# Moving the short VectorE operations of weight scales and negated maxima two steps back, behind the bank that VectorE empties

## The chip, the cores and the metric

The kernel runs on one core of a Trainium2 chip. A core has five engines with queues of their own: PE (TensorE, matrix multiplication), DVE (VectorE), ACT (ScalarE), POOL (GpSimd) and SP (SyncE, which here issues nearly all DMAs). Matmuls write into PSUM, which has eight banks; the other engines copy results from there to SBUF. The metric is the time of one execution on the device in microseconds (us). The kernel before takes 827.7 us, the median of three runs (827.12 to 828.55).

## What is computed

A layer norm, then attention with a sliding window of 256 tokens over 32 heads of 16 values, times a gate that a SwiGLU feed-forward network makes of the same normalised tokens. There are 2048 tokens of 512 values; the hidden size of the network is 1792.

```python
xn = layernorm(x)                                  # 2048 x 512
q, k, v = split(xn @ wqkv)                         # 32 heads of 16
scores = q @ k.T * 16**-0.5                        # masked: 0 <= i - j < 256
s = (softmax(scores) @ v) @ wo
g = silu((silu(xn @ w1) * (xn @ w3)) @ w2)
out = x + s * g
```

## The kernel before

Tokens are worked in four blocks of 512 (t), heads in four groups of eight (g), each group in two pairs of column sets (p): 32 units (t, g, p). Precision comes from splitting each fp32 operand into a high and a low fp16 part and summing three products (high by high, low by high, high by low). So that the fp16 parts lie in range, each weight matrix is first scaled by a power of two. The work around that scale is what the change touches:

- `squares` (L226) sums the squares of a weight tile, on ACT (L235) or DVE (L237), and casts the sums (L247).
- `powers` (L258) adds them over partitions with small matmuls (L271) into a spare part of a scores bank and returns `rest`: two operations (L280, L281) that read this bank, and three (L283, L287, L289) that make of the sum a power of two and its inverse, on tiles of 128 x 1 or 128 x 4.
- `then` (L292) runs that `rest` and what follows from it: L822 and L823 for a pair of gate and up weights, L870 to L876 for a group of down weights, where L876 writes the scale `sw`.
- With the scale known, `split_pool` (L313) cuts the raw weight: ACT scales it (L314) and casts the high part (L315), POOL subtracts for the low part (L311), in two halves. The result is stored to DRAM on SP's queue (L906, L956) for the later blocks of tokens, which load it again (L800, L846).

Attention runs in two passes. `pass1` (L605) computes scores with PE (L623) and takes their maxima on DVE (L637); after its last batch it negates the maxima of the unit into `NM` in two halves (L642, L643). `finish` (L648) later transposes these on PE (L652), DVE copies them out (L658), and SP writes them beside the queries. `pass2` (L678) computes the scores again, now with the negated maximum as two more rows (L699), adds the masks on DVE (L706), takes exponentials on ACT (L709), multiplies with the values (L727); DVE copies the sums out of PSUM (L742, L743). The denominators go through DRAM (L749, L750) and come back with the DMA of L764; DVE inverts them (L768, L769).

The dense work runs between the batches: projections (L567, emptied by L576 on ACT and L580 on DVE), gate and up products (L900, emptied by L915 on ACT, L919 and L924 on DVE), down products (L950, emptied by L974), the output product (L1001). All dense products share two PSUM banks, m0 and m1, so PE starts the next one when DVE has emptied the one before the last.

What sets the order: PE's instructions run in the order in which the kernel emits them. On the other engines a scheduler orders them by dependencies and priority when the kernel is built; each engine then runs its list strictly in order. `later(n, f)` queues the function f for n steps on; a step is counted after each batch of attention and each dense piece. `urgent` raises the priority of operations that empty PSUM. `tc.issue_after(x)` holds what it encloses behind instruction x in the list. `lasts["emptied"]` is the operation with which DVE last emptied a dense bank at the time of emission (L580, L919, L924, L971, L974 or L1005). `squares` already places its cast behind that one. Memory slots are given out in the order of the steps, so a step that is moved can change which slot a later tile gets.

Of the kernel before, what the change touches and what calls it, by code (L numbers as in the profile page):

```python
# [15 lines left out]
ALU = mybir.AluOpType  # L16
# [31 lines left out]
ONE = 2.0**12  # L48
# [31 lines left out]
def tile_block(ctx: ExitStack, tc: tile.TileContext, x, wqkv, wo, w1, w3, w2, out):  # L80
    nc = tc.nc
# [52 lines left out]
    def urgent():  # L134


        return tc.high_priority(offset=200) if started else nullcontext()
    made_so_far = [0]

    def later(n, f):  # L140
        made_so_far[0] += 1
        queue.append((now[0] + n, made_so_far[0], f))
# [21 lines left out]
    def scores_bank():  # L164

        return pss.tile([P, 2, 512], F32, name="s")
# [91 lines left out]
    def powers(sb, n, p2, inv, s=None):  # L258


        m = sb.shape[-1] // n
        al = small.tile([P, n], F32, name="al")
        if s is None:
            ps = scores_bank()[:, 0, 0:n]
            for i in range(m):
                nc.tensor.matmul(ps, onesb, sb[:, i * n:(i + 1) * n], start=i == 0, stop=i == m - 1)
        else:
            for h in range(2):
                for c in range(2):
                    for i in range(m):  # L270
                        nc.tensor.matmul(s[64 * c:64 * c + 64, h, WIN:WIN + n],  # L271
                                         onesb[64 * h:64 * h + 64, 64 * c:64 * c + 64],
                                         sb[64 * h:64 * h + 64, i * n:(i + 1) * n], start=i == 0, stop=i == m - 1)

        def rest():
            if s is None:
                nc.vector.tensor_scalar(al, ps, 2.08, 1e-30, op0=ALU.mult, op1=ALU.max)
            else:
                with urgent():
                    nc.vector.tensor_scalar(al, s[:, 0, WIN:WIN + n], 2.08, 1e-30, op0=ALU.mult, op1=ALU.max)  # L280
                    nc.vector.scalar_tensor_tensor(al, s[:, 1, WIN:WIN + n], 2.08, al, op0=ALU.mult, op1=ALU.add)  # L281

            nc.vector.tensor_scalar(al.bitcast(I32), al.bitcast(I32), 24, 23, op0=ALU.logical_shift_right,  # L283
                                    op1=ALU.logical_shift_left)
            if inv is not None:

                lasts["scale"] = nc.vector.tensor_scalar(inv.bitcast(I32), al.bitcast(I32), -1.0,  # L287
                                                         (2 * 127 - 63 + WS_EXP) * 2.0**23, op0=ALU.mult, op1=ALU.add)
            nc.vector.tensor_scalar(p2, al, 2.0**63, None, op0=ALU.mult)  # L289
        return rest  # L290

    def then(s, *made):  # L292

        def rest():
            for f in made:
                f()
        return rest if s is not None else rest()

    def scaled(a, by, name):
        t = const.tile([P, 1], F32, name=name)  # L300
# [21 lines left out]
    def weights(name, w):  # L322
# [11 lines left out]
        def scale(s=None):  # L334
            p2 = const.tile([P, 1], F32, name=f"p2{name}")
            cell["p2"], cell["sw"] = p2, const.tile([P, 1], F32, name=f"sw{name}")
            return then(s, powers(cell["sb"], 1, p2, cell["sw"], s))
# [21 lines left out]
    def weights_qk(g):  # L359
# [11 lines left out]
        def scale(s=None):  # L371
            p2 = const.tile([P, 1], F32, name=f"p2qk{g}")
            cell["p2"], cell["sw"] = p2, const.tile([P, 1], F32, name=f"sw{g}")
            return then(s, powers(cell["sb"], 1, p2, cell["sw"], s))
# [20 lines left out]
    lasts = {}  # L395
# [107 lines left out]
    def prepare_beside(t, more=0):  # L503


        load, stats, rstd, centre, turn = prepare(t)
        made = [(0, lambda b=b: load(b)) for b in range(4)]
        pairs = [(0, 1), (2, 3)] if t == 1 else [(b,) for b in range(4)]
        work = [lambda bs=bs: [stats(b) for b in bs] for bs in pairs]
        work.append(lambda: rstd(0, 4))  # L510
        work += [lambda bs=bs: [centre(b) for b in bs] for bs in pairs]
        ready = []

        def turns():

            ready.append(0)
            if len(ready) == 2:
                besides.extend(lambda s, b=b, n=n: turn(b, n, s) for b in range(4) for n in (0, 2))
        work.append(turns)
        made.append((0, lambda: later(more, lambda: behind.extend(work))))  # L520
        return made, turns
# [26 lines left out]
    def keys(t, g):  # L548
        return KA[(t * NG + g) % 3]
# [55 lines left out]
    def pass1(t, g, p):  # L605


        M = small.tile([P, 2, 2, 4], F32, name="M")
        whole = NM[(2 * (t * NG + g) + p) % len(NM)]
        nm = whole[:, 0:32].rearrange("p (b i) -> p b i", b=2)  # L610

        def part(ii, a, beside, narrow):
            qa, ka = QA[t, g], keys(t, g)
            i = t * 4 + ii
            n, mask = ((i + 1) * P, M1.rearrange("p a b -> p (a b)")[:, (1 - i) * P:]) if i < 2 else (WIN, MW)
            s = pso.tile([P, 2, TW], F32, name="po") if beside else scores_bank()

            w = 32 if narrow else 64
            for c in range(0, P, w):
                e = (ii + 3) * P if i < 2 else (ii + 2) * P + 64 * (c // 64 + 1)  # L620
                for r in range(2):
                    rows = slice(64 * r, 64 * r + KR)
                    nc.tensor.matmul(s[c:c + w, r, :n], qa[rows, 2 * p + a, ii * P + c:ii * P + c + w],  # L623
                                     ka[rows, 2 * p + a, e - n:e], start=True, stop=True)
            after = []
            if narrow:
                pass
            elif alone[0] and maxima and (ii, a) != (0, 0):
                after = [f(s) for f in maxima]
                maxima.clear()  # L630
            elif alone[0] and besides:
                after = [besides.pop(0)(s)]
            alone[0] = not after or t * NG + g <= 2
            for r in range(2):
                junk = ppool.tile([P, D], BF16, name="junk", bufs=1)
                with urgent():
                    lasts["maximum"] = nc.vector.tensor_tensor_reduce(  # L637
                        out=junk[:, :n], in0=s[:, r, :n], in1=mask, scale=1.0,
                        scalar=NEG, op0=ALU.add, op1=ALU.max, accum_out=M[:, r, a, ii:ii + 1])
            if (ii, a) == (3, 1):  # L640
                Mf = M.rearrange("p r a i -> p (r a i)")
                nc.vector.tensor_scalar(nm[:, 0, :], Mf, -1.0 / ONE, None, op0=ALU.mult)  # L642
                nc.vector.scalar_tensor_tensor(nm[:, 1, :], Mf, -1.0 / ONE, nm[:, 0, :], op0=ALU.mult, op1=ALU.subtract)  # L643
                maxima.append(finish)
            for f in after:
                f()

        def finish(s):  # L648

            for h in range(2):  # L650
                rows = slice(64 * h, 64 * h + 64)
                nc.tensor.matmul(s[0:64, h, 448:512], whole[rows, 0:64], identh[rows, rows], start=True, stop=True)  # L652

            def rest():
                qa = QA[t, g]
                mt = small.tile([32, P], F16, name="mt")
                with urgent():
                    nc.vector.tensor_copy(mt.rearrange("p (h q) -> p h q", h=2), s[0:32, :, 448:512])  # L658
                dm = dpool.tile([32, P], F16, name="dm")
                nc.sync.dma_start(dm, mt)  # L660
                for r in range(2):
                    nc.sync.dma_start(qa[64 * r + KR:64 * r + KR + 2, 2 * p:2 * p + 2, :].rearrange("p a q -> p (a q)"),
                                      dm.rearrange("(b r i) q -> r b (i q)", b=2, r=2)[r])
            return rest
        return [lambda *kind, ii=ii, a=a: part(ii, a, *kind) for ii in range(4) for a in range(2)]

    def last_maxima():
# [612 lines left out]
    for n, u in enumerate(units):  # L1280
        if n == 0:
            first, second = prepare_beside(1, 2)
# [52 lines left out]
```

## Time and profile before

| | |
|---|---|
| runs, us | 827.12, 827.7, 828.55 |
| span of the profiled execution, first to last instruction, us | 824.7 |
| mean granted clock of TensorE | 0.996 |
| busy, us (share of the span): PE | 803.9 (97%) |
| DVE | 632.2 (77%) |
| ACT | 388.8 (47%) |
| POOL | 205.6 (25%) |
| idle time of POOL's L311 behind ACT's L929 | 406.9 |
| idle time of ACT's L709 behind DVE's L706 | 196.4 |
| DMA | 110.66 MB, mean 134 GB/s |

The profile tells for every instruction when the engine ran it, and for idle time which semaphore ended it. The profiled execution's own device time stands beside no row; its span lies 3.0 us under the median of the runs. Large idle times of POOL and ACT are not by themselves a cost. A line such as `107.83 0.56 DVE L643 ...` in the timeline says: from 107.83 us, for 0.56 us, DVE worked on line 643; `out<-in` are tile names with partitions x elements; `x2` are two instructions in a row; brackets give the idle time just before and what ended it. Line numbers are those of the kernel before.

### The profile page before, as it was taken

How to read it: one execution, taken by the hardware profiler on the slowest of the kernel's cores; microseconds unless marked ns; L12 is line 12 of the kernel's file. 1: busy time of each engine (PE TensorE's matmuls, PEld its weight loads, DVE VectorE, ACT ScalarE, POOL GpSimd, SP SyncE). 2: the span in 40 equal slices, each digit the busy share in tenths (PEclk: the TensorE clock that was granted, in tenths of full speed). 3: DMA queues.
4: the chain of work that ended last, by engine and by line, in shares of the span. 5: the costliest groups of instructions: out<-in, count | busy, mean ns of one | idle time of the engine just before them, and what ended most of it. 6: DMA issues, size and time to landing. Idle time of an engine off the chain costs nothing. (4 is left out here: it accounts for less than half of the span.)

```text
span 824.7 us, 22891 instructions
## 1 busy us (share of the span) xinstructions
PE 803.9 (97%) x8924; PEld 380.7 (46%) x8924; DVE 632.2 (77%) x2021; ACT 388.8 (47%) x562; POOL 205.6 (25%) x355
## 2 busy tenths in 40 slices
PE   8999989999999999999999999999999999999998
PEld 4434435444445444444444444444444444444444
DVE  8788878887798678879878887778777787676435
ACT  6889775634435434344343444442433344343511
POOL 2238174332223203121211111230201113030201
PEclk9999989999999999999999999999999999999999
DMA  9978566266543354544433344434434353343101
GB/s 283 267 230 237 194 177 191 73 170 186 160 122 84 98 154 124 161 117 135 134 105 100 108 109 138 132 119 113 142 85 144 91 131 102 101 132 91 56 21 53
DMA packets 95325, 110.66 MB, mean 134 GB/s; under 512 B 17200, under 2 KB 60528, under 8 KB 95216
## 3 DMA queue, kind: packets, MB, share of 16 engines
q1 hardware_dynamic: 94928, 108.67, 45.9%
q8 instruction: 70, 1.15, 0.6%
q10 hardware_dynamic: 288, 0.52, 0.2%
q14 instruction: 39, 0.32, 0.1%
HBM read 76.28 MB, written 28.57 MB: 127 GB/s over the span
## 5 line engine op out<-in xcount | busy, mean ns | idle before, releaser
L311 POOL TENSOR_TENSOR slot<-slot,slot 128x256 f16<-128x256 f32 (+1 forms) x228 | 151.1, 690 | 522.3 <-ACT slot L929 406.9
L900 PE MATMUL m<-XH,slot 128*128 128x512 f16 x896 | 269.0, 382 | 6.3 <-DVE slot L924 3.2
L709 ACT ACTIVATE pt<-s,es 128x1024 f32<-128x1024 f32 x152 | 167.7, 1113 | 198.3 <-DVE s L706 196.4
L900 PEld LDWEIGHTS <-slot 128*128 128x128 f16 x1344 | 125.4, 98 | 162.6 <-issue 18.9
L900 PE MATMUL m<-XL,slot 128*128 128x512 f16 x448 | 170.5, 381 | 0.0
L950 PE MATMUL m<-slot,slot 128*128 128x512 f16 x672 | 156.5, 380 | 1.5 <-DVE slot L580 0.7
L706 DVE TENSOR_TENSOR s<-s,MK 128x256 f32<-128x256 f32 (+2 forms) x280 | 118.3, 435 | 49.4 <-PE s L699 47.0
L637 DVE CUSTOM_DVE_ANT_0 junk<-s,MW 128x320 bf16<-128x320 f32 x276 | 134.1, 486 | 24.6 <-PE s L623 15.8
L950 PEld LDWEIGHTS <-slot 128*128 128x128 f16 x672 | 61.9, 98 | 79.7 <-issue 9.0
L637 DVE CUSTOM_DVE_ANT_0 junk<-po,MW 128x320 bf16<-128x320 f32 x172 | 83.6, 486 | 5.4 <-DVE al L283 0.5
L727 PE MATMUL po<-pt,V 64*32 64x320 f32 (+4 forms) x2880 | 77.2, 342 | 0.1
L929 ACT CAST slot<-slot 128x512 f16<-128x512 f32 x56 | 34.5, 616 | 76.0 <-DVE slot L924 71.8
L915 ACT ACTIVATE slot<-m,sgs 128x512 f32<-128x512 f32 x56 | 38.3, 684 | 54.9 <-PE m L900 54.8
L727 PEld LDWEIGHTS po<-pt,V 64*32 64x32 f32 x2880 | 51.1, 106 | 21.6 <-issue 0.8
L919 DVE SCALAR_TENSOR_TENSOR slot<-slot,m 128x512 f32<-128x512 f32 x56 | 38.3, 684 | 27.6 <-ACT slot L915 27.3
L699 PE MATMUL s<-qa,KA 50*64 50x320 f16 (+3 forms) x1472 | 58.3, 260 | 0.6 <-ACT pt L709 0.6
L699 PEld LDWEIGHTS <-KA 50*64 50x64 f16 x1472 | 30.3, 106 | 55.3 <-issue 32.7
L623 PE MATMUL s<-KA,qa 48*64 48x320 f16 (+3 forms) x824 | 45.5, 295 | 4.3 <-ACT pt L709 3.2
L924 DVE SCALAR_TENSOR_TENSOR slot<-m,slot 128x512 f32<-128x512 f32 x56 | 38.5, 687 | 10.6 <-PE m L900 10.0
L974 DVE SCALAR_TENSOR_TENSOR slot<-m,dsc,slot 128x512 f32<-128x512 f32 x48 | 35.9, 747 | 13.2 <-PE m L950 13.0
L567 PE MATMUL m<-XH,whi 128*128 128x512 f16 x120 | 44.7, 381 | 0.0
L567 PE MATMUL m<-XL,whi 128*128 128x512 f16 x120 | 44.5, 379 | 0.0
(162 smaller groups left out, 870.6 us busy)
## 6 DMA issues: line engine op xcount, KB each, us to landing
slot<-dW SPq DMA_DIRECT2D x126, 256.0 KB
slot<-in_B_w_dram SPq DMA_DIRECT2D x42, 256.0 KB
dW<-slot SPq DMA_DIRECT2D x42, 256.0 KB
slot<-in_A_x_dram SPq DMA_DIRECT2D x30, 256.0 KB
KA<-dK SPq DMA_DIRECT2D x24, 288.0 KB
qa<-dQ SPq DMA_DIRECT2D x32, 192.0 KB
dQ<-slot SPq DMA_DIRECT2D x16, 256.0 KB
dK<-slot SPq DMA_DIRECT2D x16, 256.0 KB
```

The costliest lines, as they stand in the source:

```text
L311: op(out[:, c], a[:, c], b[:, c])
L567: nc.tensor.matmul(cell["pp"], a[:, k, c, :], b[:, c, :], start=(c, i) == parts[0][0], stop=(c, i) == parts[-1][-1])
L623: nc.tensor.matmul(s[c:c + w, r, :n], qa[rows, 2 * p + a, ii * P + c:ii * P + c + w], ka[rows, 2 * p + a, e - n:e], start=True, stop=True)
L637: lasts["maximum"] = nc.vector.tensor_tensor_reduce(out=junk[:, :n], in0=s[:, r, :n], in1=mask, scale=1.0, scalar=NEG, op0=ALU.add, op1=AL ...
L699: nc.tensor.matmul(s[64 * h:64 * h + 64, r, o:o + 64 * n], ka[rows, 2 * p + a, 64 * (m + 4):64 * (m + 5)], qa[rows, 2 * p + a, 64 * (m + k ...
L706: nc.vector.tensor_add(v, v, MK[:, kind, of:of + n, :].unsqueeze(1).to_broadcast([P, 2 * len(which), n, 64]))
L709: nc.scalar.activation(pt, s, AF.Exp, scale=es)
L727: nc.tensor.matmul(cell["po"][32 * i:32 * i + 32, h, 64 * (m + k):64 * (m + k + n)], V[64 * h:64 * h + 64, (4 * t + m // 2) % VB, hd * VW: ...
L900: nc.tensor.matmul(cell[k], w[:, (a * NC + c) * P:(a * NC + c + 1) * P], b[:, c, :], start=c == 0 and i == 0, stop=c == NC - 1 and i == 2)
L915: nc.scalar.activation(sg, cell[0], AF.Tanh, scale=sg_scale[:, f:f + 1])
L924: lasts["emptied"] = nc.vector.scalar_tensor_tensor(sg, cell[1], 0.5 * HS / (WS * XS)**2, sg, op0=ALU.mult, op1=ALU.mult)
L950: nc.tensor.matmul(ps, hh[:, a * TW + b * P:a * TW + (b + 1) * P], w[:, c * D:(c + 1) * D], start=f == f0 and i == 0, stop=f == f1 - 1 and ...
```

## The change

`powers` now returns two functions: `rest`, the two operations that read the scores bank, and `chain`, the operations that follow. `then` runs the first at its old time and queues the others two steps later, behind the dense bank that DVE empties last by then. Whatever the chain itself queues (the cuts of weights) counts its steps from there. `pass1` queues the negation of the maxima in the same way. Where no scores bank is handed in (`s` is None, at the start of the kernel), all runs at once as before.

```diff
+        def chain():
             nc.vector.tensor_scalar(al.bitcast(I32), al.bitcast(I32), 24, 23, op0=ALU.logical_shift_right,
                                     op1=ALU.logical_shift_left)
             if inv is not None:
...
             nc.vector.tensor_scalar(p2, al, 2.0**63, None, op0=ALU.mult)
-        return rest
-
-    def then(s, *made):
-
-        def rest():
-            for f in made:
+        return rest, chain
+
+    def then(s, read, *made):
+
+        first, *rest = *(read if isinstance(read, tuple) else (read,)), *made
+
+        def chain():
+            for f in rest:
                 f()
-        return rest if s is not None else rest()
+
+        def behind_bank():
+            with tc.issue_after(lasts["emptied"].ins) if "emptied" in lasts else nullcontext():
+                chain()
+
+        def now_and_later():
+            first()
+            later(2, behind_bank)
+        if s is not None:
+            return now_and_later
+        first()
+        chain()
...
             if (ii, a) == (3, 1):
-                Mf = M.rearrange("p r a i -> p (r a i)")
-                nc.vector.tensor_scalar(nm[:, 0, :], Mf, -1.0 / ONE, None, op0=ALU.mult)
-                nc.vector.scalar_tensor_tensor(nm[:, 1, :], Mf, -1.0 / ONE, nm[:, 0, :], op0=ALU.mult, op1=ALU.subtract)
+                later(2, negate)
                 maxima.append(finish)
             for f in after:
                 f()
+
+        def negate():
+            Mf = M.rearrange("p r a i -> p (r a i)")
+            with tc.issue_after(lasts["emptied"].ins):
+                nc.vector.tensor_scalar(nm[:, 0, :], Mf, -1.0 / ONE, None, op0=ALU.mult)
+                nc.vector.scalar_tensor_tensor(nm[:, 1, :], Mf, -1.0 / ONE, nm[:, 0, :], op0=ALU.mult, op1=ALU.subtract)
```

## The prediction

> **What bounds the kernel now.** I read the page first, then the busy time by stages, then what TensorE waited for, then the timeline around each place that the change touches.
>
> ```profile
> span 824.7 us, 22891 instructions
> ...
> 56.00:222.00 166.00, 157.58 (x1676) 74.41 (x1679) 132.96 (x487) 107.86 (x187) 70.11 (x122) 0.98 0.59 178
> 222.00:740.00 518.00, 515.46 (x6197) 245.14 (x6198) 411.19 (x1280) 212.79 (x257) 103.14 (x160) 1.00 0.42 118
> 740.00:824.70 84.70, 80.39 (x755) 38.26 (x752) 43.58 (x88) 24.32 (x30) 14.57 (x22) 1.00 0.20 61
> ```
>
> The stage rows give the stretch, its length, then the busy time of PE, weight loads, DVE, ACT and POOL, the granted clock, the DMA share and GB/s. From 222 to 740 us PE is busy 515.5 of 518.0 us: nothing can be won there, and a stall is lost in full. From 56 to 222 us, the stage in which weights are scaled and cut, PE is idle 8.4 us. That is the room for a gain. What ended those waits:
>
> ```profile
> engine line waited for: us in total, times, longest us
> PE m L900 <- DVE slot L924: 3.2, 1, 3.2
> PE s L623 <- ACT pt L709: 3.2, 3, 1.3
> PE m L900 <- DVE slot L580: 1.6, 2, 1.4
> ```
>
> One stall of 3.2 us stands out: PE wants a PSUM bank that DVE (L924) has not emptied. The change speaks to exactly that.
>
> **What is moved.** Nothing is added or removed. Built, the changed program has the same instructions on every engine, and the same order on PE and POOL. The listing of DVE shows 16 of the 32 pairs of negated maxima (L642, L643) eight to ten instructions later and the other 16 where they were; of the 15 chains of scales (L283 on) only two stand visibly later, one for a group of down weights (L870 to L876), one for a pair of gate and up weights (L822, L823). But the cuts of the weights hang on these chains, so 23 places of ACT's order and 21 of SP's change too, nearly all ahead of 270 us, and some slots are given to other tiles.
>
> **The stall that goes (T1).**
>
> ```profile
> 106.88 5.43 POOL L311 TENSOR_TENSOR slot<-slot,slot 128x256 f16<-128x256 f32 x8
> ...
> 107.83 0.56 DVE L643 SCALAR_TENSOR_TENSOR NM<-M,NM 128x16 f16<-128x16 f32 x1
> ...
> 109.20 0.63 DVE L283 TENSOR_SCALAR al<-al 128x4 int32<-128x4 int32 x1
> ...
> 111.11 0.16 DVE L872 TENSOR_REDUCE q<-pp 128x1 f32<-128x4 f32 x1
> ...
> 111.69 0.65 DVE L876 TENSOR_SCALAR sw<-p,q 128x4 f32<-128x4 f32 x1
> ...
> 112.37 1.33 ACT L314 ACTIVATE slot<-slot,sw 128x512 f32<-128x512 f32 x2 [4.05 <-DVE sw L876]
> 112.96 0.62 DVE L743 TENSOR_TENSOR os<-os,po 128x448 f32<-128x448 f32 x1
> 113.50 0.68 DVE L924 SCALAR_TENSOR_TENSOR slot<-m,slot 128x512 f32<-128x512 f32 x1
> ...
> 114.24 1.01 PE L900 MATMUL m<-XH,slot 128*128 128x512 f16 x2 [3.25 <-DVE slot L924]
> ```
>
> Seven short operations run from 109.20 to 112.34, ahead of the copies of L742 and L743 and of L924. In the new order they stand behind all three. Those start 3.1 us earlier, L924 ends near 111.1 instead of 114.18, and PE is free at 110.99: the gap goes but for 0.0 to 0.3 us. T1 = -3.2 us.
>
> **The scales that come late (T2).** The chain gives the scale sw, for which ACT's cuts, POOL's second halves and the stores on SP's queue wait.
>
> ```profile
> 115.05 1.64 DVE L449 TENSOR_SCALAR slot<-slot,mv,rs 128x512 f32<-128x512 f32 x2
> ...
> 117.16 0.90 SPq L956 DMA_DIRECT2D dW<-slot  x2
> ...
> 118.17 0.44 SPq L764 DMA_DIRECT2D dr<-dd  x1
> ...
> 123.19 0.35 DVE L768 RECIPROCAL dr<-dr 128x32 f32<-128x32 f32 x1 [0.91 <-DMA dr<-dd]
> ...
> 124.49 0.69 DVE L580 SCALAR_TENSOR_TENSOR slot<-m,slot 128x512 f16<-128x512 f32 x1 [0.48 <-ACT slot L576]
> ...
> 126.29 0.59 PE L900 MATMUL m<-XH,slot 128*128 128x512 f16 x2
> ```
>
> What now comes first on DVE ended near 115.2 and slides forward by the freed 3.7 us (3.14 and L643's 0.56), to 111.5. Then come the pair, the seven and the two L449 among them. With the durations above that is 5.9 us with gaps, and sw is done at 117.4. With the nine short ones at the 0.16 of L872, an estimate, it is 3.3 us: 114.8. Against 112.34, sw is 2.5 to 5.1 us late. I take 3.5 (done at 115.8), because POOL, beside which the short ones are long, has its run of L311 ended at 112.31.
>
> From sw to the first store: two ACT passes (1.33), a cast (0.6), two POOL halves (2 x 0.68), 3.3 us in all. L956 goes at 119.2, and right behind it, on the same queue, L764, which loads the softmax denominators: 119.7 instead of 118.17 (118.6 to 121.2). Its landing here took 5.0 us (118.17 to 123.17); the shortest in the trace is this one:
>
> ```profile
> 485.63 0.33 SPq L764 DMA_DIRECT2D dr<-dd  x1
> ...
> 487.62 0.35 DVE L768 RECIPROCAL dr<-dr 128x32 f32<-128x32 f32 x1 [0.36 <-DMA dr<-dd]
> ```
>
> That is 2.0 us. I take the middle, 3.5, as fewer transfers stand before it in the new queue: landing at 123.2 (120.6 to 126.2). DVE sits on L768 until then, and behind it on DVE are L769, a cast, a mask and the bank emptier L580: 0.35, 0.42, 0.17, 0.42, 0.69, so 2.05 us, to 125.25. PE, now 3.2 us ahead, wants that bank at 123.05 instead of 126.29. The stall that T1 removed comes back as 2.2 us (0 to 5.2). Behind it the exponentials queue on ACT after the late cuts, and the masks behind L768; the row of L623 waiting for L709 shows that PE does feel such a queue. I add 0.5 (0 to 1.2).
>
> The same shift in the other early chains: a POOL half behind PE's L950 or an exponential a few tenths late. I add 0.5, between -0.5 (part of the 1.4 before L580 goes) and +0.8.
>
> **The order on SP at 253 us (T3).**
>
> ```profile
> 252.16 3.81 POOL L311 TENSOR_TENSOR slot<-slot,slot 128x256 f16<-128x256 f32 x6 [0.44 <-ACT slot L315]
> ...
> 253.45 2.43 SPq L749 DMA_DIRECT2D on<-os  x4
> ...
> 256.84 0.34 SPq L800 DMA_DIRECT2D slot<-dW  x1
> ...
> 257.63 0.34 SPq L764 DMA_DIRECT2D dr<-dd  x1
> ...
> 260.70 0.35 DVE L768 RECIPROCAL dr<-dr 128x32 f32<-128x32 f32 x1
> ...
> 263.28 0.31 PE L623 MATMUL po<-KA,qa 48*64 48x320 f16 x4
> ```
>
> Here the load of L800 gets another slot, one that POOL's cut of wo frees, and stands ahead of the four L749. It can go at 252.16 + 3.81 = 255.97, so L749 goes at 256.3, 2.9 us late, and L764 at 260.5. With the 3.07 us between its rows it lands at 263.6; then L768 (0.35) and a maximum (0.43 and 0.08) before the po bank is free: 264.4 against PE's 263.28, 1.1 us. With a landing of 2.0 us it is nothing; with what piles up behind, 1.9. I take 1.1, this place's own row.
>
> **The last pair (T4).**
>
> ```profile
> 750.02 1.47 PE L950 MATMUL m<-slot,slot 128*128 128x512 f16 x6
> 750.13 0.17 DVE L643 SCALAR_TENSOR_TENSOR NM<-M,NM 128x16 f16<-128x16 f32 x1
> ...
> 751.13 0.69 DVE L743 TENSOR_TENSOR os<-os,po 128x512 f32<-128x512 f32 x1
> 751.42 0.22 PE L652 MATMUL s<-identh,NM 64*64 64x64 f16 x2
> ...
> 751.74 0.74 DVE L974 SCALAR_TENSOR_TENSOR slot<-m,dsc,slot 128x512 f32<-128x512 f32 x1
> ```
>
> L652 transposes the last maxima, at once after the batch. The pair now stands behind L974, which cannot start before L950 ends at 751.49; it ends at 752.25, the pair (2 x 0.17 and gaps) near 752.65, and PE stands from 751.42: +1.2 us (1.0 to 1.3). Nothing hides it.
>
> **The other pairs (T5).**
>
> ```profile
> L642 DVE TENSOR_SCALAR NM<-M x32: 157/174/627, 45.3 to 749.9; 128x16 f16<-128x16 f32 x32
> L643 DVE SCALAR_TENSOR_TENSOR NM<-M,NM x32: 151/174/599, 45.5 to 750.1; 128x16 f16<-128x16 f32 x32
> ```
>
> ```profile
> 298.77 0.18 DVE L643 SCALAR_TENSOR_TENSOR NM<-M,NM 128x16 f16<-128x16 f32 x1
> ...
> 304.07 0.19 PE L652 MATMUL s<-identh,NM 64*64 64x64 f16 x2
> ```
>
> A pair takes 0.35 us, and PE asks for it 5.1 us later. Eight instructions further back cost some 3.5 us of that: covered with 1.6 us left, so nothing. The bank that is emptied 0.35 us sooner is worth nothing either, as PE does not wait in this stage. Without the cover each of the 16 would cost what T4 does.
>
> **Sum.** -3.2 + 2.2 + 0.5 + 0.5 + 1.1 + 1.2 = +2.3 us. The span goes from 824.7 to 827.0. The median of the runs, 827.7, lies 3.0 us above the profiled span (launch and end lie around it), so the forecast is **830.0 us**.
>
> **Rivals.** A, *not slower*: the denominators land before DVE asks. The place is L768 near 120.5 us; the price is the whole of T2; it decides at a landing by 121. With sw at 114.8 and L764 at 118.6, a landing of 2.0 to 2.4 us does it. Then T2, its tail and T3 are 0, the early term -0.5, and -3.2 - 0.5 + 1.2 = -2.5: 825.2 us. For it: L283 and L876 are long just while POOL runs, L872 is not. Against: a landing of 5.0 at this very place. The Trainium skill, "SBUF — State Buffer", section "SBUF: two separate sides", says the same in other words: GpSimd and certain VectorE operations share one pair of ports, whoever starts first holds it for the whole instruction, and the other is blocked. By that rule the moved operations are short wherever POOL is idle; L643 between 151 and 599 ns agrees.
>
> B, *much slower*: sw at 117.4 and a landing of 5.0. T2 is 5.2, its tail 1.2, the early term 0.8, T3 1.9: -3.2 + 5.2 + 1.2 + 0.8 + 1.9 + 1.2 = +7.1, 834.8 us. For it: these are the rows' own durations. Against: the queue before L764 is emptier than before.
>
> C, *no change*: the stall only moves. The scheduler left 13 of 15 chains and half the pairs in place; if T1 and T2 with its tail cancel and the rest is hidden, T4 alone is left: 828.9 us.
>
> **Chances.** Forecast 0.43, A 0.20, B 0.20, C 0.17. 0.2% is 1.65 us, about what a measurement of this kernel can tell from no change: A falls under 826.05, C inside, B above; of the forecast's own range, 828.8 to 832, a little (0.03) lies inside. So faster 0.20, same 0.20, slower 0.60. The range leaves out the lower half of A and the upper half of B: 825.5 to 834.0.
>
> **What would show it.** Right: no wait for L924 of over 1 us on PE near 111; L768 with some 3 us of idle time before it near 120 to 124, and PE waiting for L580 behind it; L749 leaving 3 us late after an L800 near 256; PE waiting about 1.2 us for L643 at the last L652. Wrong: L768 without idle time (then A), PE waiting in the steady stage for pairs (T5 uncovered), or the 3.2 us still there.

## The result and the profile after

The changed kernel takes 824.93 us, the median of 13 runs (823.39 to 827.29); the kernel before took 827.7 in 13 runs beside it (825.51 to 829.24). The ratio is 0.9972, with an interval of 0.9962 to 0.9982: faster by 0.28%, where a loss of 0.3% was forecast. The profiled execution lasts 823.93 us, 1.8 us more than its span of 822.1; in each of the 13 runs the time lies 1.8 us above the span, to within 0.1. By that the profiled execution of before lasted some 826.5 us, 1.2 under the median; the prediction's 3.0 us between span and median are these two together.

The lines have moved in the numbering after: L924 is L942, L919 is L937, L900 is L918, L580 is L594, L567 is L581, L642 and L643 are L663 and L664, L652 is L670, L709 is L727, L749 is L767, L764 is L782, L768 is L786, L800 is L818, L876 is L894, L956 is L974, L974 is L992.

The busy time by the same three stages, their bounds shifted to the same matmuls, to within four small ones (columns as before: stretch, length, busy time of PE, weight loads, DVE, ACT and POOL, granted clock, DMA share, GB/s):

```profile
55.60:217.60 162.00, 155.51 (x1672) 73.69 (x1671) 132.62 (x486) 108.44 (x188) 71.03 (x124) 1.00 0.59 183
217.60:736.30 518.70, 515.56 (x6197) 245.30 (x6198) 412.50 (x1282) 213.12 (x257) 103.30 (x160) 1.00 0.41 118
736.30:822.10 85.80, 80.39 (x754) 38.24 (x752) 43.71 (x88) 24.31 (x30) 14.57 (x22) 0.99 0.19 60
```

The stage in which weights are cut became 4.0 us shorter, the other two 0.7 and 1.1 longer. Its granted clock rose from 0.98 to 1.00, and PE is idle 6.5 us of it instead of 8.4. So in this stage less than half of the gain is idle time that went; the rest is matmuls that ran faster.

PE's waits after the change (line of PE and line waited for; us in total, times, longest):

```profile
PE s L670 <- DVE NM L664: 1.8, 3, 1.1
PE m L918 <- DVE slot L937: 1.7, 3, 0.8
PE s L637 <- ACT pt L727: 1.6, 4, 0.7
...
PE m L581 <- DVE slot L937: 0.7, 1, 0.7
```

The stall of 3.2 us is not there. Nothing of its size took its place. New are the waits for L664 (1.1 us for the last pair, 0.46 near 112 us); those for L937 (L919 of before, 1.4 us then) grew to 2.4.

The program order on PE is the same in both kernels, so each matmul can be compared with itself. First the stretch of 36 matmuls that held the stall and the 125 matmuls that follow, before:

```profile
110.00:119.91 9.91, 6.67 (x36) 2.42 (x35) 7.77 (x22) 7.51 (x14) 7.93 (x13) 0.66 0.72 227
119.91:130.00 10.09, 10.09 (x125) 5.19 (x124) 8.27 (x37) 8.34 (x18) 2.37 (x4) 1.00 0.72 219
```

and the same matmuls after:

```profile
109.46:114.05 4.59, 4.13 (x36) 1.91 (x35) 4.49 (x17) 2.31 (x3) 3.81 (x6) 1.00 0.88 304
114.05:126.65 12.60, 10.86 (x125) 5.29 (x124) 10.15 (x43) 11.69 (x22) 6.44 (x10) 1.00 0.58 185
```

The first stretch lost 5.3 us, not 3.2: the idle time fell from 3.24 to 0.46, and the busy time of the same 36 matmuls from 6.67 to 4.13, as the granted clock went from 0.66 to 1.00. In the trace of before the clock is at one half from 113.08 to 119.91 us. The second stretch gave 2.5 us back: PE, busy for all of it before, now has 1.74 us of idle time there and 0.77 us more of busy time. The two belong together: a matmul of 512 columns is drawn 0.38 us long, but in an unbroken run the next one starts 0.21 us after it, so the first 0.17 us of each wait count as busy. For the price of a wait I therefore compare the starts of the same matmuls.

The place itself, in the timeline after (start, duration, engine, line, operation, tiles; idle time before it and what ended it):

```profile
107.81 5.46 POOL L325 TENSOR_TENSOR slot<-slot,slot 128x256 f16<-128x256 f32 x8
...
109.31 0.68 DVE L942 SCALAR_TENSOR_TENSOR slot<-m,slot 128x512 f32<-128x512 f32 x1
...
111.13 0.16 DVE L284 TENSOR_SCALAR al<-al 128x4 int32<-128x4 int32 x1
...
112.02 0.64 DVE L664 SCALAR_TENSOR_TENSOR NM<-M,NM 128x16 f16<-128x16 f32 x1
112.71 0.22 PE L670 MATMUL s<-identh,NM 64*64 64x64 f16 x2 [0.46 <-DVE NM L664]
113.47 0.15 DVE L888 TENSOR_TENSOR pp<-pp,p 128x4 f32<-128x4 f32 x1
...
114.24 0.23 DVE L894 TENSOR_SCALAR sw<-p,q 128x4 f32<-128x4 f32 x1
114.50 1.33 ACT L328 ACTIVATE slot<-slot,sw 128x512 f32<-128x512 f32 x2 [1.97 <-DVE sw L894]
...
115.11 0.38 PE L581 MATMUL m<-XH,whi 128*128 128x512 f16 x1 [0.67 <-DVE slot L937]
...
118.17 0.38 SPq L782 DMA_DIRECT2D dr<-dd  x1
119.96 0.35 DVE L786 RECIPROCAL dr<-dr 128x32 f32<-128x32 f32 x1 [2.20 <-DMA dr<-dd]
...
121.36 0.68 DVE L594 SCALAR_TENSOR_TENSOR slot<-m,slot 128x512 f16<-128x512 f32 x1
121.56 0.38 PE L918 MATMUL m<-XL,slot 128*128 128x512 f16 x1
122.09 0.59 PE L918 MATMUL m<-XH,slot 128*128 128x512 f16 x2
```

L942 now ends at 109.99, 4.2 us earlier. The scale sw is done at 114.47, 2.1 us later than before, and the denominators' load (L782) leaves at the same clock time as before, 118.17. It lands by 119.96, in 1.8 us where it took 5.0. DVE does sit 2.20 us on L786. The matmul that wants L594's bank starts at 122.09, 0.05 us after L594 ends and 0.53 instead of 0.21 us after the matmul before it: PE does wait there, by 0.3 us.

The end:

```profile
748.63 0.17 DVE L664 SCALAR_TENSOR_TENSOR NM<-M,NM 128x16 f16<-128x16 f32 x1
748.86 0.22 PE L670 MATMUL s<-identh,NM 64*64 64x64 f16 x2 [1.14 <-DVE NM L664]
```

Where the time went, by the start of the same matmul, minus its start before (worked out from the two traces; times are those of before):

```text
us before   62     110    119.9   130    168    200    262    300    745    760    end
shift      -0.44  -0.54  -5.86  -3.35  -3.86  -4.38  -4.26  -3.71  -3.76  -2.56  -2.6
```

### The profile page after: what moved, and what is told of

Its sections match the earlier page's. It is cut to its first block, busy times and chain, and to the rows that moved or that the text cites. A ratio compares the mean times of both kernels' runs of the same rounds, so it can differ in the third digit from the quotient of the medians.

```text
span 822.1 us, 22902 instructions
## 1 busy us (share of the span) xinstructions
PE 802.3 (98%) x8924; PEld 380.1 (46%) x8924; DVE 633.5 (77%) x2021; ACT 389.4 (47%) x562; POOL 205.9 (25%) x355
## 3 DMA queue, kind: packets, MB, share of 16 engines
q8 instruction: 70, 1.15, 0.6%
## 5 line engine op out<-in xcount | busy, mean ns | idle before, releaser
L325 POOL TENSOR_TENSOR slot<-slot,slot 128x256 f16<-128x256 f32 (+1 forms) x228 | 151.5, 691 | 518.5 <-ACT slot L947 391.9
L918 PE MATMUL m<-XH,slot 128*128 128x512 f16 x896 | 267.3, 380 | 3.1 <-DVE slot L937 1.7
L727 ACT ACTIVATE pt<-s,es 128x1024 f32<-128x1024 f32 x152 | 167.7, 1113 | 194.4 <-DVE s L724 192.5
L918 PEld LDWEIGHTS <-slot 128*128 128x128 f16 x1344 | 125.1, 98 | 158.1 <-issue 14.0
L918 PE MATMUL m<-XL,slot 128*128 128x512 f16 x448 | 169.8, 379 | 0.0
L717 PE MATMUL s<-qa,KA 50*64 50x320 f16 (+3 forms) x1472 | 58.2, 259 | 1.2 <-ACT pt L727 0.6
L937 DVE SCALAR_TENSOR_TENSOR slot<-slot,m 128x512 f32<-128x512 f32 x56 | 38.3, 685 | 23.4 <-ACT slot L933 23.2
L717 PEld LDWEIGHTS <-KA 50*64 50x64 f16 x1472 | 30.2, 105 | 55.6 <-issue 34.0
L637 PE MATMUL s<-KA,qa 48*64 48x320 f16 (+3 forms) x824 | 45.4, 294 | 2.9 <-ACT pt L727 1.6
L942 DVE SCALAR_TENSOR_TENSOR slot<-m,slot 128x512 f32<-128x512 f32 x56 | 38.5, 688 | 10.6 <-PE m L918 10.1
L992 DVE SCALAR_TENSOR_TENSOR slot<-m,dsc,slot 128x512 f32<-128x512 f32 x48 | 35.9, 748 | 13.4 <-PE m L968 13.1
L581 PE MATMUL m<-XH,whi 128*128 128x512 f16 x120 | 44.7, 381 | 1.1 <-DVE slot L937 0.7
L581 PE MATMUL m<-XL,whi 128*128 128x512 f16 x120 | 44.5, 379 | 0.0
```

What stands on the lines that cost most here:

```text
L325: op(out[:, c], a[:, c], b[:, c])
L581: nc.tensor.matmul(cell["pp"], a[:, k, c, :], b[:, c, :], start=(c, i) == parts[0][0], stop=(c, i) == parts[-1][-1])
L717: nc.tensor.matmul(s[64 * h:64 * h + 64, r, o:o + 64 * n], ka[rows, 2 * p + a, 64 * (m + 4):64 * (m + 5)], qa[rows, 2 * p + a, 64 * (m + k ...
L727: nc.scalar.activation(pt, s, AF.Exp, scale=es)
L918: nc.tensor.matmul(cell[k], w[:, (a * NC + c) * P:(a * NC + c + 1) * P], b[:, c, :], start=c == 0 and i == 0, stop=c == NC - 1 and i == 2)
L942: lasts["emptied"] = nc.vector.scalar_tensor_tensor(sg, cell[1], 0.5 * HS / (WS * XS)**2, sg, op0=ALU.mult, op1=ALU.mult)
```

## The experiments

Each ratio is to runs of the kernel before on the same chip (medians 827.45 for the first four, 827.79 for the next four, 828.15 for the last three). A profile shows one execution; that of the steps alone (825.55 us) was the fastest of its kernel, that with all squares held (830.36) the slowest. The edits are against the changed kernel. Lines shift by a few from kernel to kernel; the operation tells which is which. In the expectations, M is the theory that the stall in front of the bank emptier at 111 us, with the half clock behind it, is the whole gain and that the chain of the down weights alone takes it away; Q is the theory that ACT's queue decides as well.

### The chains alone

```diff
-                later(2, negate)
+                Mf = M.rearrange("p r a i -> p (r a i)")
+                nc.vector.tensor_scalar(nm[:, 0, :], Mf, -1.0 / ONE, None, op0=ALU.mult)
+                nc.vector.scalar_tensor_tensor(nm[:, 1, :], Mf, -1.0 / ONE, nm[:, 0, :], op0=ALU.mult, op1=ALU.subtract)
```

> Only the chains of scales are moved, the negated maxima stay at once behind their batch. Theory M (the gain is one place: the stall of 3.25 us at 111 us and the half clock of 6.8 us behind it go, because the scale chain of the down weights stands behind L924): all of the gain stays and the last pair's 1.1 us comes back, so 1.1 us below the changed kernel, about 823.8 us, no PE wait over 1 us for L924 near 111, clock 1.0 there. Rival R (the pairs of negated maxima, out of the way of the banks in every unit, make the gain): close to the kernel before, 827 us or more. By-product: the pair at 105-112 us stands ahead of L924 again, which may leave a wait of some 0.5 us.

Measured: 823.78 us (823.63 to 824.93), ratio 0.9955 (0.994 to 0.997). This is the lowest median of all; it lies 1.15 us under the changed kernel's, but the intervals of the two ratios overlap. Its waits and its windows at the old stall:

```profile
PE m L920 <- DVE slot L939: 1.4, 3, 0.5
```

```profile
111.00:114.00 3.00, 2.84 (x31) 1.36 (x30) 2.97 (x12) 2.05 (x3) 2.33 (x4) 1.00 1.01 358
```

No stall, full clock, and no wait for the last pair. The chains carry the gain; the maxima add nothing to it.

### The maxima alone

```diff
-            later(2, behind_bank)
+            chain()
```

> Only the negated maxima are moved, the chains run at once. Theory M: the seven short operations still stand ahead of L924, so PE still waits 2.5 to 3.3 us near 111 (less by the 0.56 us of the pair at most), the clock drops to 0.5 behind it for some 5 to 7 us, and the last pair costs 1.1: 827.7 + 1.1 - 0.6 = 828.2 us, not below 827. Rival R: about 825 us.

Measured: 827.61 us, ratio 1.0009 (0.9998 to 1.0021).

```profile
PE m L918 <- DVE slot L942: 2.6, 1, 2.6
```

```profile
115.00:118.40 3.40, 2.47 (x24) 1.04 (x23) 2.72 (x5) 3.40 (x7) 3.40 (x6) 0.50 0.65 180
```

The stall stays at 2.6 us, shorter by the pair that no longer stands in front, and the clock still falls to 0.50. The steady stage shows no loss from the other pairs: the shift is 0.11 us at 168 and -0.21 at 745.

### The last pair at once

```diff
-                later(2, negate)
+                if (t, g, p) == units[-1]:
+                    ...
+                else:
+                    later(2, negate)
```

> The changed kernel with the pair of the last unit alone negated at once. If PE's wait of 1.14 us at the last L652 is what the late pair costs: 1.1 us below the changed kernel, 823.8 us, span 821.0, and no wait of L652 for the pair at the end. Rival: the time is hidden or another wait takes its place (the copies of L742, L743 and L974 that now run before the pair): no change, 824.9 us.

Measured: 824.16 us, ratio 0.9961 (0.9947 to 0.9974). Between 745 and 760 us the shift stays at -2.25, where the changed kernel loses 1.20: the wait at the last transposition is the last pair's alone. The medians differ by 0.8 us (824.93 and 824.16), with intervals that overlap.

### Two steps later, without the order behind the bank

```diff
-            with tc.issue_after(lasts["emptied"].ins) if "emptied" in lasts else nullcontext():
-                chain()
+            chain()
...
-            with tc.issue_after(lasts["emptied"].ins):
+            with nullcontext():
```

> Everything is emitted two steps later as in the change, but not held behind the bank. In the listing the chain of the down weights then stands ahead of L924 again. Theory M: stall of about 3 us near 111 and half clock behind it are back, 827 to 828 us. Rival S (the later cuts, with the other order on ACT and SP, make the gain, not the place behind the bank): about 825 us.

Measured: 826.97 us, ratio 0.9988 (0.9978 to 0.9999).

```profile
PE m L917 <- DVE slot L941: 2.7, 1, 2.7
```

Without the order, the stall is back at 2.7 us, and the clock is at one half for 3.4 us behind it. It is the order, not the two steps, that frees the bank. The scale sw is not late here (its last operation starts at 110.58 us; 111.69 before, 114.24 after the change), so rival S, that the later cuts make the gain, is not tested by this run.

### The chains of the down weights alone

```diff
-    def then(s, read, *made):
+    def then(s, read, *made, late=False):
...
-            later(2, behind_bank)
+            if late:
+                later(2, behind_bank)
+            else:
+                chain()
...
-            return then(s, powers(sb, n, p2, None, s), lambda: rest(p2))
+            return then(s, powers(sb, n, p2, None, s), lambda: rest(p2), late=True)
```

In this kernel and in all that follow, the maxima are negated at once, as in the first.

> Only the chains of the down weights are moved; those of gate, up and other weights and the maxima run at once. Theory M (the one chain ahead of L924 and the half clock behind its stall): the whole gain is there, 823.5 to 824.5 us, clock 1.0 from 105 to 125. Rival P (the later chains of gate and up weights, with the other order on ACT and SP, carry a part): 825.5 us or more.

Measured: 827.52 us, ratio 1.0 (0.9989 to 1.0011). M missed by 3 us. The stall in front of the bank did go, but PE now waits longer in another place:

```profile
PE s L640 <- ACT pt L732: 7.4, 4, 4.1
```

```profile
113.46 0.63 ACT L235 ACTIVATE sqa<-slot 128x512 bf16<-128x512 f32 x1 [3.71 <-DMA slot<-in_B_w_dram]
...
115.87 0.63 ACT L881 ACTIVATE sqa<-slot 128x512 bf16<-128x512 f32 x1 [1.18 <-DMA slot<-in_B_w_dram]
116.50 1.09 ACT L732 ACTIVATE pt<-s,es 128x1024 f32<-128x1024 f32 x1
117.64 0.32 PE L640 MATMUL s<-KA,qa 48*64 48x128 f16 x4 [4.15 <-ACT pt L732]
```

```profile
116.60:123.30 6.70, 5.66 (x23) 2.08 (x23) 5.10 (x21) 6.70 (x12) 2.61 (x5) 0.50 0.26 87
```

Two sums of squares on ACT (L235, L881) wait for their weights, 3.71 and 1.18 us, and the exponential (L732) for which PE waits stands behind them in the same queue. PE waits 4.15 us, and the clock falls to 0.50 for 6.8 us.

### The other chains alone

The same edit with `late=True` in the place of the gate and up pairs, and not in that of the down weights.

> The other half: the chains of gate and up weights are moved, those of the down weights run at once, ahead of L924. Theory M: no gain, 827 to 828 us, a PE wait of about 3.2 us for L924 near 111 and half clock behind it. Rival P: 826 us or less.

Measured: 825.66 us, ratio 0.9978 (0.9967 to 0.9989).

```profile
PE m L923 <- DVE slot L947: 3.3, 1, 3.3
```

The whole stall and its half clock are there, and the kernel is still 2.1 us faster than before. The shift falls from 0.47 at 130 us to -2.03 at 200: these chains win later, among other things at a wait of 1.32 us at 165 that is gone. M has no room for this, and rival P held.

### Half of the chain

```diff
             first()
+            if late == "half":
+                rest.pop(0)()
+            if late:
+                later(2, behind_bank)
+            else:
+                chain()
```

Late are only the down weights' last operations (L870 to L876 of before).

> Of the down weights' chain the first two operations stay ahead of L924 and the last five (L870 to L876) are moved. The stall is left at 3.25 less the five and their gaps (2.1 to 2.2 us), so 1.0 to 1.3 us. Theory M, with the clock as a cost of its own that a stall this short does not bring: clock 1.0 throughout, and only that 1.0 to 1.3 us over the kernel with the whole chain moved, about 825.2 us. Rival N (no cost but the wait itself; what the half clock lost is made up later): about 827 us, as only two thirds of the 3.25 us are saved and the later waits give back 1 to 2.5. If the clock drops behind 1.2 us too, M's bound on when it drops is wrong.

Measured: 827.78 us, ratio 1.0002 (0.9989 to 1.0014).

```profile
PE s L642 <- ACT pt L734: 6.4, 4, 3.2
...
PE m L925 <- DVE slot L949: 1.4, 1, 1.4
```

The stall is 1.4 us, with two of the chain's seven operations still in front, and the clock stays up behind it. But the wait for an exponential is there as in the kernel with the down chains alone, 3.2 us, and behind that the clock is at one half for 3.4 us. The time is the one that rival N gave, but it contains this other wait, so it does not decide between M and N.

### Work that nobody needs, in front of the bank

Kernel one (chains late, maxima at once), and in the old place of the down weights' second chain a copy and three reciprocals of 128x128 that nothing reads. Nothing is left out.

```diff
+            made = then(s, powers(sb, n, p2, None, s), lambda: rest(p2))
+            if k != 1:
+                return made
+
+            def filled():
+                made()
+                fill = const.tile([P, 128], F32, name="fill")
+                nc.vector.tensor_copy(fill, s[:, 0, 0:128])
+                for _ in range(3):
+                    nc.vector.reciprocal(fill, fill)
+            return filled
```

> The kernel with all chains moved, and at the old place of the second down chain a copy and three reciprocals of 128 x 128 (about 2.9 us by the 0.35 us of 128 x 32 and the 0.16 of 128 x 1) that nothing needs, ahead of L924. Theory M: a stall of 2.5 to 3.2 us near 111 is back, the clock drops to 0.5 behind it, and the time is 827 to 829 us though the cuts of weights come as late as in the change. Rival L (the later cuts and the order on ACT and SP make the gain): 824 to 825 us.

Measured: 824.61 us, ratio 0.9958 (0.9937 to 0.9978).

```profile
113.38 0.59 PE L930 MATMUL m<-XH,slot 128*128 128x512 f16 x2 [2.00 <-DVE slot L954]
```

```profile
113.40:116.80 3.40, 3.25 (x32) 1.52 (x32) 3.33 (x14) 2.27 (x3) 1.30 (x2) 1.00 0.56 194
```

A stall of 2.00 us is put back, the clock stays at 1.00, and the median lies only 0.8 us above the first kernel's. From 110 to 130 us the shift goes from 0.39 to -1.90, in the first kernel from -0.43 to -3.10: of the 2.0 us, 0.4 are left. The stall came out shorter than M asked for and brought no half clock, so M's case did not arise; the time lies in rival L's range, and that the later cuts have a share in the gain is not excluded by it.

### The down chains alone, with two squares held back

The kernel with the down chains alone, and the two squares on ACT ordered behind the exponential:

```diff
-        nc.scalar.activation(sq, RAW2[f], AF.Square, accum_out=NORMS[k][:, f - f0:f - f0 + 1])
+        with tc.issue_after(lasts["exp"].ins) if f in (10,) else nullcontext():
+            nc.scalar.activation(sq, RAW2[f], AF.Square, accum_out=NORMS[k][:, f - f0:f - f0 + 1])
```

and the same around the 32nd square of `squares`.

> As e5 (only the chains of the down weights moved), but two of ACT's sums of squares, the ones that in e5 stood ahead of an exponential and waited for weights still being loaded, are held behind that exponential. Theory Q (in e5 the stall only changed its place: PE waits 4.15 us for an exponential behind squares that wait for a load): that wait shrinks to under 1 us, the clock stays 1.0, and the gain that e5 lacked appears: 824 to 825.5 us. Rival (the late scales themselves make the exponential late, or PE is held by something else there): the wait stays over 2 us, 827 us or more.

Measured: 825.12 us (824.9 to 826.0), ratio 0.9966 (0.9952 to 0.9979).

```profile
112.43 1.11 ACT L737 ACTIVATE pt<-s,es 128x1024 f32<-128x1024 f32 x1 [0.19 <-DVE s L734]
```

The exponential runs at 112.43 instead of 116.50, the long wait is gone (the longest left for an exponential, 1.9 us near 164, is another one), the clock is full, and the median lies 2.4 us under that of the down chains alone, with intervals of the two ratios that don't meet. Q held. So the down chains bring their gain only where ACT's queue is in an order that suits them; in the changed kernel it is the other chains' shift that puts it so, as the kernel with all chains, which differs from that with the down chains only in the others, has no such wait.

### More of the work that nobody needs

The kernel with work that nobody needs, now with four reciprocals, made urgent.

> As e8 with four reciprocals (0.94 us each there) ahead of L924 instead of three. The stall near 111 grows from 2.0 to about 2.9 us. If the half clock is a cost of its own that sets in between those lengths (2.0 brought none in e8, 2.6 brought it in e2 and e4): the clock drops to 0.5 for one or two stretches of 3.4 us, and the time grows by 0.9 + 1 to 2.4, to 826.5 to 828 us. If only the wait itself counts: 825.5 us.

Measured: 828.4 us, ratio 1.0002 (0.9989 to 1.0014).

```profile
PE m L931 <- DVE slot L955: 2.8, 1, 2.8
PE s L719 <- ACT pt L729: 1.7, 2, 1.2
PE po L637 <- DVE XL L511: 1.3, 1, 1.3
```

```profile
115.00:118.00 3.00, 2.55 (x29) 1.19 (x29) 3.00 (x11) 2.12 (x3) 1.30 (x2) 1.00 0.36 100
...
154.60:158.00 3.40, 3.21 (x11) 1.18 (x12) 3.33 (x16) 1.74 (x2) 1.30 (x2) 0.50 0.01 2
```

The stall of 2.8 us leaves the clock at 1.00 behind it. The half clock comes 40 us later, behind two waits of 1.2 and 1.3 us. Of the loss, 3.7 us fall between 130 and 168 (shift -1.26 to 2.46), so the time of this kernel says nothing about the stall at 111 us. It isn't a clean test of the stall's price.

### All squares held back

The first kernel, with every square on ACT behind the last exponential.

> As e1 (all chains moved, maxima at once), with every sum of squares on ACT held behind the exponential emitted last. If the small waits of PE for exponentials in e1 (1.7 us in five waits) come from squares that stand ahead of them: 0.5 to 1.2 us below e1, 822.6 to 823.3. If the squares, now late, hold up their casts and the sums of the scales on PE: e1's time or slower, 824 to 826.

Measured: 827.06 us, ratio 0.9992 (0.9981 to 1.0004), a miss.

```profile
PE s L272 <- DVE sb L248: 4.3, 2, 2.3
```

Now PE waits twice, up to 2.3 us, for the sums of squares themselves (L248), and behind each the clock falls to one half, at 74.43 and at 125.63 us. Two squares held at the right place helped; all of them are too many.

## Why the prediction was wrong

By the prediction's own terms, each measured as a difference of the shifts above (us):

```text
term                                        forecast   measured
early chains                                 +0.5     -1.57 (-0.54 to 110 us, -1.03 from 130 to 200)
T1, the stall                                -3.2     -5.32 (110 to 119.9)
T2 with its tail, the late scale             +2.7     +2.51 (119.9 to 130), 0.31 of it at L594
from 200 to 262 (no term)                     0       +0.12
T3, SP's order near 253 us                   +1.1     +0.55 (262 to 300)
T5, the other pairs (300 to 745)              0       -0.05
T4, the last pair                            +1.2     +1.20
sum                                          +2.3     -2.56
```

The steps that failed are T1 and the early term, 2.1 us each. The forecast priced the stall at its own 3.2 us and at nothing more, and it took the early chains as a loss. Rival A's 825.2 us came close to the 824.93 by luck: its -3.2 and -0.5 were each too small a gain, and its nothing for T2 and T3 too small a loss.

**T1.** The direction was right, the size not. The row 56.00:222.00 in the prediction shows a granted clock of 0.98, while the other two stages show 1.00; two hundredths of 166 us were 3.3 us of clock that the working did not use. They are the stretch at one half from 113.08 to 119.91, which begins inside the stall. In the profiled executions the same 36 matmuls were busy 2.5 us less after the change, and PE was idle 2.8 us less among them (3.24 less the new 0.46 behind L664).

How much of that reaches the end is not settled, and the evidence is on both sides. In the profiles, the shift from 110 to 130 us sorts by the clock: -2.3 to -2.8 in the four kernels without stall and without half clock at this place (after, the first, the third, the down chains with two squares held); -2.3 and -2.4 in the two with 2.0 and 2.8 us of stall and a full clock (the two kernels with unneeded work); -0.5 to 0.8 in the three with a stall of 2.6 to 3.3 and the clock at one half (maxima alone, steps alone, other chains alone). But each execution that was timed has its mean clock too, and of the 80 of the kernel before that ran beside the experiments, 11 show 1.000, which leaves no room for a step of 3.4 us at one half (that takes the mean to 0.998); their mean is 827.8 us, no better than the medians of the three groups (827.45, 827.79 and 828.15). Among the other 69 the time does rise as the clock falls: 826.0 us in the mean at 0.999, 827.4 at 0.998, 828.1 at 0.996, 829.1 at 0.995. But the eight executions of the changed kernel at 1.000 have a mean of 825.1, so the gain is 2.7 us also where neither kernel shows a half clock. The half clock accounts for T1 in the profile; the gain of the median is not shown to come from it, and what else makes those eleven slow stays open.

**T2.** The chain of events was right up to the load and wrong behind it. sw was done at 114.47 (forecast 115.8): five of the chain's seven operations, from L888 at 113.47 to L894, run when POOL's run of L325 has ended (107.81 + 5.46 = 113.27), and the first and last of them take 0.15 and 0.23 us, where L870 and L876 took 0.58 and 0.65 before, beside POOL. That is close to the low estimate, 114.8, that the prediction worked out and then left for a middle value. The load left at 118.17 (119.7) and landed within 1.8 us, outside the bounds of 2.0 to 5.0. DVE sat idle 2.20 us in front of L786, but nearly all of that lay before PE asked for the bank: at the place that the prediction priced with 2.2 us, PE lost 0.31. The rest of the 2.5 us came in four other places, by the starts of the same matmuls: 0.83 at L581 behind L937, 0.51 at L637 behind L727, 0.45 at L717 behind L281 and 0.38 at L637 behind L511. So the number came near by luck. Rival A was right that the landing comes by 121 us, but not that DVE would not wait for it. What made the landing short (1.8 against 5.0 us) was not tried.

**Early chains.** Forecast as a loss, they won 1.6 us. The prediction let the late cuts push exponentials back on ACT, and read PE's waits of L623 for L709 (3.2 us, the longest 1.3) only as a sign that more would be lost. The largest single gain shows the reverse. Before:

```profile
164.68 0.61 ACT L315 CAST slot<-slot 128x512 f16<-128x512 f32 x1
165.20 1.11 ACT L709 ACTIVATE pt<-s,es 128x1024 f32<-128x1024 f32 x1
...
166.35 0.25 PE L623 MATMUL s<-KA,qa 48*64 48x128 f16 x4 [1.32 <-ACT pt L709]
```

and after:

```profile
159.34 1.11 ACT L727 ACTIVATE pt<-s,es 128x1024 f32<-128x1024 f32 x1 [0.19 <-DVE s L724]
161.44 1.33 ACT L328 ACTIVATE slot<-slot,pi 128x512 f32<-128x512 f32 x2 [0.98 <-DVE pi L288]
```

Before, the exponential stood behind the cuts of a pair of gate and up weights; now their scale comes later, the exponential goes first, and PE's wait is gone (shift -2.53 to -4.02). The other chains alone bring the same at this place (0.19 to -1.31) and win 2.5 us between 130 and 200 us, with the stall untouched. Earlier, the wait at 56 us fell from 1.44 to 1.0 us, as far as the prediction's low bound went, and that at 91 us from 1.20 to 0.19; the latter was nearly used up by 0.9 us of losses at 68 and 78 us.

**T3.** At its place the mechanism was right: the load of L818 does stand ahead of L767.

```profile
251.75 0.34 SPq L818 DMA_DIRECT2D slot<-dW  x1
252.19 2.42 SPq L767 DMA_DIRECT2D on<-os  x4
...
256.36 0.34 SPq L782 DMA_DIRECT2D dr<-dd  x1
...
258.05 0.35 DVE L786 RECIPROCAL dr<-dr 128x32 f32<-128x32 f32 x1 [1.53 <-DMA dr<-dd]
...
262.84 0.42 PE L717 MATMUL s<-qa,KA 50*64 50x320 f16 x12 [0.33 <-DVE XL L511]
```

L782 leaves at 256.36, 3.0 us later than before by its matmuls (257.63 less the shift of 4.3), as forecast. It lands in 1.7 us instead of 3.07. By the prediction's own words a landing of 2.0 us costs nothing at the po bank, and PE does start on it at 259.02 without a wait. The 0.55 us were lost elsewhere: 0.15 at L918 and 0.41 at L717, which waits for L511, behind DVE's 1.53 us of idle time at L786. Where L767 stands first, as in the maxima alone and the other chains alone, nothing is lost there. So the order on SP was right, the place of the loss was not.

**T4 and T5.** Both held. PE waits 1.14 us for the last pair, forecast 1.2; the kernel with the last pair at once has no such wait. The other pairs cost nothing from 300 to 745 us (-0.05).

**The tests the prediction named.** No wait of over 1 us near 111: seen. Idle time in front of the denominators' reciprocal: seen, 2.2 us for some 3. PE waiting for L594 behind it: seen, but with 0.3 us instead of 2.2. L767 3 us late: seen. A wait at the last transposition: seen.

**What the runs add.** That the order behind the bank removes the stall is shown (two steps alone: stall back); the ratio of that kernel, 0.9988, lies clear of the chains alone, while its interval just touches that of the changed kernel. That the down chains alone are not enough, as the stall moves to ACT's queue, is shown by the pair of kernels with and without the two squares held, 827.52 and 825.12. That the other chains win by themselves is shown by the kernel that moves only them. The maxima alone bring no gain, and the last pair behind the bank costs 1.2 us in the profiles of the two kernels that have it there (after, and the maxima alone) and nothing in the first and the third. Not settled are the price of the half clock without a stall, and whether the later cuts have a share.

## What to carry to other kernels

Short operations that nobody awaits belong behind the copy that empties a bank; but those whose reader asks at once (here the last pair) belong in front, and the version that moves only the chains has the lowest median, 823.78 us, though its interval overlaps that of the changed kernel. For each stall read the granted clock behind it and every wait in the stage, not only the longest one, before pricing its removal. And look up where the stall can go: an in-order queue (here ACT's) with an instruction that waits for a load ahead of one that PE needs turned a gain of 2.4 us into nothing.

## What the runs showed of the hardware

**The clock.** The granted clock went to one half in steps of 3.413 us, one or two steps long, at times on a grid of that length through the whole execution. What decided was how much of one step of the grid PE was idle, not how long the stall was. Sorted over the profiles of all 13 kernels, without the last 10 us of each:

```text
idle time of PE in one step of 3.41 us             clock behind it
3.06 2.54 2.35 2.35 2.33 2.26 2.26 2.09 1.99       one half
1.74 1.65 1.64 1.63 1.62 1.61 and all below        full
```

In the last 10 us, 2.10 us and more brought the drop, but one step with 1.99 us, in the kernel before, left none behind it, so the bound lies near 2 us. The stall of 2.81 us with four reciprocals fell on two steps, 1.51 and 1.62, and left the clock up; the stall of 2.6 us of the maxima alone fell in one and did not. The Trainium skill, "TensorE: Matmul & The Clock Gate", section "What's actually happening", tells of a free-running window of 3413 ns: the grid agrees. Its section "HAM oscillation — how this bites in real kernels" gives the rule that gaps of PE over about 3.4 us bring the drop; here gaps of 2.6 and 3.25 us did, and the measurement decides.

**Short DVE operations beside POOL.** They are longer beside POOL in many places and not in all. L664 took 0.64 us at 112.02, while POOL worked on L325, and 0.17 at 748.63; but L284 took 0.16 at 111.13 with POOL running, and the three operations of before's chain on 128x1 tiles (L872 to L874) took 0.15 to 0.16 beside it as well. A single price for such an operation, which the prediction looked for, does not exist. In the profiles before and after, none on tiles of 128x1 to 128x16 took over 0.23 us away from POOL, and those on 128x1 were short beside it too; what sets the rest from one instruction to the next was not tried.
